# Block-sparse attention and a feed-forward layer on one core: sparse scores with fewer, wider matmuls, and another pace for the feed-forward work

## The chip, the core and the metric

The kernel runs on one core of a Trainium2 chip. A core has TensorE (PE in the profile; its loads of the stationary operand are PEld), VectorE (DVE), ScalarE (ACT), GpSimd (POOL) and SyncE (SP), which run their own instruction streams and wait for each other by semaphores, and 16 DMA engines. The metric is the device time of one execution in microseconds (us), the median over runs.

## The reference

Four batches, eight heads, 768 tokens, head size 64; the tokens form 24 blocks of 32. A query block sees its own block and its two neighbours, the first and the last block, and three sampled blocks; the first and the last query block see everything. A layer norm and a feed-forward layer with residual follow.

```python
scores = scale * np.matmul(q, k.transpose(0, 1, 3, 2))
mask = np.abs(blk_i - blk_j) <= window
mask = mask | (blk_i == 0) | (blk_j == 0) | (blk_i == n_blocks - 1) | (blk_j == n_blocks - 1)
for qb in range(n_blocks):
    for kb in sampled_blocks[qb]:
        mask[qb * block:(qb + 1) * block, kb * block:(kb + 1) * block] = True
attn = softmax(np.where(mask, scores, -1e9))
x = attn @ v                                     # heads joined: 768 x 512 per batch
xn = (x - mu) / np.sqrt(var + 1e-06) * g_ln
out = x + np.maximum(xn @ w_ch1, 0.0) @ w_ch2    # 512 -> 2048 -> 512
```

Inputs are float32. The kernel splits each operand into a high and a low float16 part, so most products are three matmuls: high by high, high by low, low by high.

## The kernel before, in words

**Steps.** Attention works on query tiles t of 128 tokens (four query blocks), 0 to 5 in each of the four batches b, and on half the heads at a time (hg, four heads). One such pair is a sparse step; there are 48. Twice per batch and half two dense steps compute the first and the last query block against all keys. All 64 steps are numbered in program order. A sparse step:

- `gather_k` (L273) copies the keys of the 12 sampled blocks on ACT into a tile `kg`, out of the converted keys `kx`; both come from a pool of three buffers. It is issued two steps ahead.
- `scores` (L317) writes the step's scores, `ps`: 128 partitions, 4 heads, 256 columns each, which are three near blocks (columns 0 to 95), the first and the last block (96 to 159) and three sampled blocks (160 to 255). The four query blocks have different near and sampled keys, so each query block and head has a matmul of its own for each of the three pieces, with 32 queries as the stationary operand: 96 matmuls, 48 with the low query part `ql` (64 contraction rows, two heads side by side) and 48 with the high part `qx` (128 rows, where the other 64 hold the keys' low part).
- `softmax_max`, `softmax_exp`, `split_high` and `split_low` (DVE, ACT) make the probabilities' high and low parts `pw`, and two DMA transposes turn them into `pt`.
- `gather_v` brings the values into `vg`, by DMAs on SP and by indirect DMAs on POOL; `attn_v` (L431) multiplies, two steps later (LAG), into `pa`; `finish` divides.

**Units.** Two query tiles of a batch are a unit, in the order (1, 2), (3, 4), (0, 5); there are 12. When both are finished, `layer_norm` normalises them on DVE and ACT and brings them, turned by DMA, into `xT`. `ffn` (L519) is a generator: 192 matmuls up (`pu`, L532), 96 down (`pd`, L561). Below, U and D are such matmuls, up and down.

**Order.** Nothing is scheduled by a tool: the program order of each engine is that of the main loop (L792). Each turn i issues the scores of step i, the exponentials, the values of step i - 2, and between these, in eight parts (`go`), matmuls of the feed-forward generators. `quota` (L805) says how many: what is still to be done (`need`), divided by the turns until the next unit comes in (`avail`), at most `CAP` = 78. So the feed-forward work of one unit ends as the next unit comes in. Steps 0 to 7 (NPE) have another order and turn the probabilities on PE; then the weights are converted as well.

Of the kernel before, what the change touches and what calls it, by code (L numbers as in the profile page):

```python
# [10 lines left out]
F16 = mybir.dt.float16  # L11
# [15 lines left out]
def sparse_attention_moe(  # L27
# [13 lines left out]
    nc = tc.nc  # L41
    P = 128
    B, NT = qs.shape[0], qs.shape[1]
    H = 8
    D = 64
    HG = 2
    HL = H // HG
    BLK = 32
    NB = NT * 4
    NR = 3  # L50
# [7 lines left out]
    LAG, FFLAG, CAP = 2, 1, 78  # L58
# [1 line left out]
    FFU = 192 + 2 * 16 * 6  # L60

    const = ctx.enter_context(tc.tile_pool(name="const", bufs=1))
    kp = ctx.enter_context(tc.tile_pool(name="kp", bufs=3))
    rawp = ctx.enter_context(tc.tile_pool(name="rawp", bufs=3))
    wfp = ctx.enter_context(tc.tile_pool(name="wfp", bufs=3))
    qp = ctx.enter_context(tc.tile_pool(name="qp", bufs=3))
# [29 lines left out]
            name=nc.get_next_instruction_name(), act_func_set_id=ACT_SET, ins=[], outs=[]  # L96
# [72 lines left out]
    def convert_w(i):  # L169
# [16 lines left out]
        def to_high():  # L186
# [5 lines left out]


    kxs, vgs, qxs, kgs = {}, {}, {}, {}
    vdr = {(b, hg): dr.tile([(NB + 1) * BLK, VW], F16, name=f"vdr{b}_{hg}")
           for b in range(B) for hg in range(HG)}
    vsb = [const.tile([P, H, VR], F16, name="vs")]
# [21 lines left out]

    def convert_k(b, hg, c):  # L220
        if c == 0:
            kxs[b, hg] = kp.tile([P, 2, NB, HL // 2, BLK], F16, tag="kx", name=f"kx{b}_{hg}")
        kx, raw = kxs[b, hg], raws.pop(("k", b, hg, c))
        at = slice(c * NB // 2, (c + 1) * NB // 2)
        for j in range(2):
            rows, other = slice(j * D, (j + 1) * D), slice((1 - j) * D, (2 - j) * D)
            nc.scalar.copy(kx[rows, j, at], raw[rows])
            nc.vector.tensor_sub(kx[other, j, at], raw[rows], kx[rows, j, at])
            yield
# [43 lines left out]
    def gather_k(s):  # L273
        b, t, hg = s.b, s.t, s.hg
        if hg == 0:
            _, got = nc.values_load_multi_w_load_instructions(
                regs[0:1, t * 4 * NR : (t + 1) * 4 * NR], engines=(ET.Activation,), min_val=0,
                max_val=NB - 1,
                skip_runtime_bounds_check_because="every sampled block is a block's number")
            vals[b, t] = got  # L280
        kg = kp.tile([P, 4 * NR, 2, HL // 2, BLK], F16, tag="kg", name=f"kg{b}_{t}_{hg}")
        kgs[b, t, hg] = kg
        for n, val in enumerate(vals[b, t]):
            nc.scalar.copy(kg[:, n], kxs[b, hg][:, :, bass.ds(val, 1)].rearrange("p j o q k -> p j (o q) k"))  # L284
            if n % 4 == 3:
                yield

# [29 lines left out]
    def scores(s):  # L317
        kx, (qx, ql) = kxs[s.b, s.hg], qxs[s.b, s.t]
        kg = kgs[s.b, s.t, s.hg]
        s.ps = ps_s.tile([P, 2, 2, 2 * P], F32, tag="ps", name=f"ps{s.i}")  # L320

        def segments(gr, hl):
            qb = 4 * s.t + gr
            w = min(max(qb - 1, 0), NB - 3)
            j, q = hl % 2, hl // 2
            yield 0, 3, kx[:, j, w : w + 3, q, :]
            yield 3, 2, kx[:, j, 0 : NB : NB - 1, q, :]
            yield 5, 3, kg[:, NR * gr : NR * (gr + 1), j, q, :]

        def put(gr, j, pr, rows, stat, first, last):  # L330
            dst = s.ps[gr * BLK : (gr + 1) * BLK, j, pr, :].rearrange("p (b k) -> p b k", k=BLK)
            for at, n, src in segments(gr, 2 * pr + j):
                nc.tensor.matmul(dst[:, at : at + n], stat, src[rows], start=first, stop=last,  # L333
                                 skip_group_check=True)
                first = False

        for pr in range(2):
            for gr in range(4):
                for j in range(2):
                    rows = slice(j * D, (j + 1) * D)  # L340
                    put(gr, j, pr, rows, ql[rows, 2 * s.hg + pr, gr * BLK : (gr + 1) * BLK],
                        pr == 0, False)
        for pr in range(2):
            for j in range(2):
                for gr in range(4):
                    put(gr, j, pr, slice(0, P), qx[:, j, 2 * s.hg + pr, gr * BLK : (gr + 1) * BLK],
                        False, True)

    def dense_scores(s):
        kx = kxs[s.b, s.hg]  # L350
# [270 lines left out]
    def place(n):  # L621
        return n + (1 if n < NPE else LAG)

    def matmul_scores(s):
        (dense_scores if s.dense else scores)(s)
# [35 lines left out]
    def keys(i):  # L661
        if i < NS and not steps[i].dense and i not in gathered:
            gathered.add(i)
            work(gather_k(steps[i]))
# [48 lines left out]
    first = ORDER[0]  # L713
# [13 lines left out]
    for c in range(2):  # L727
        work(convert_k(0, 0, c))
# [12 lines left out]
    for b in range(1, B):  # L741
        f = next(s.i for s in steps if s.b == b)
        k0, v0 = max(f - 13, NPE + 1), max(f - 11, NPE + 1)
        for hg, i in ((0, k0), (1, f - 4)):
            for c in range(2):
                item(i + c, "b", "raw", lambda b=b, hg=hg, c=c: load_k(b, hg, c),
                     lambda b=b, hg=hg, c=c: convert_k(b, hg, c))
        for kt in range(NT):
            item(v0 + kt, "d", "raw", lambda b=b, kt=kt: load_v(b, kt), lambda b=b, kt=kt: convert_v(b, kt))
# [10 lines left out]
    for n, s in enumerate(order):  # L760
# [4 lines left out]
        else:  # L765
            old = order[n - 3]
            i = place(old.i + 1 if old.dense else old.i)
# [18 lines left out]
    avail = {}  # L786
    for u in units:
        last = max(s.i for s in steps if s.u is u)
        avail[u.i] = last + 2 - 100 * (u.i == 0) if last < NPE else last + LAG + FFLAG
    need = 0  # L790
    i = 0
    while i < NS + LAG + FFLAG + 1 or ffq:  # L792
        s = steps[i] if i < NS else None
# [9 lines left out]
        later = [a for a in avail.values() if a > i]  # L803

        def quota():  # L805
            return min(-(-need // (min(later) - i)), CAP) if later else need

        nff = quota()
        part = [nff * (k + 1) // 8 - nff * k // 8 for k in range(8)]
        wready.update(wdone[: len(wdone) - 1 if i < NPE else None])  # L810
        hook(i, "pre")
        if i < NPE:
# [5 lines left out]
            if i == 0:  # L818
                convert_w(0)
                work(convert_k(0, 1, 0))  # L820
                split_high(s)
                high()
# [53 lines left out]
        else:  # L876
# [3 lines left out]
            def go(k):  # L880
                nonlocal need
                if k == 4:
                    begin(True)
                    if i >= NPE:
                        nff = quota()
                        for m in range(4, 8):
                            part[m] = nff * (m + 1) // 8 - nff * m // 8
                n = part[k]
                for m in range(2):
                    need -= run(n * (m + 1) // 2 - n * m // 2)  # L890
                    low()
                    tick()
                    high()
# [106 lines left out]
```

## Time and profile before

| | |
|---|---|
| time, median of 3 runs | 848.17 us (842.59 to 858.56) |
| the profiled execution | 842.86 us, its span 841.1 us |
| PE matmuls busy | 700.7 us, 13776 matmuls and as many loads |
| DVE, ACT, POOL busy | 496.1, 467.8, 175.6 us |
| mean granted TensorE clock | 0.941 |

Busy time of an engine is the time in which at least one of its instructions ran; small matmuls that run side by side count once. The chain of work is followed back from the last instruction through whatever released each one. "issue" in it is time in which an engine waited for nothing that the profile shows.

### The profile page before, as it was taken

How to read it: one execution, taken by the hardware profiler on the slowest of the kernel's cores; microseconds unless marked ns; L12 is line 12 of the kernel's file. 1: busy time of each engine (PE TensorE's matmuls, PEld its weight loads, DVE VectorE, ACT ScalarE, POOL GpSimd, SP SyncE). 2: the span in 40 equal slices, each digit the busy share in tenths (PEclk: the TensorE clock that was granted, in tenths of full speed). 3: DMA queues.
4: the chain of work that ended last, by engine and by line, in shares of the span. 5: the costliest groups of instructions: out<-in, count | busy, mean ns of one | idle time of the engine just before them, and what ended most of it. 6: DMA issues, size and time to landing. Idle time of an engine off the chain costs nothing.

```text
span 841.1 us, 31767 instructions
## 1 busy us (share of the span) xinstructions
PE 700.7 (83%) x13776; PEld 475.5 (57%) x13776; DVE 496.1 (59%) x900; ACT 467.8 (56%) x1201; POOL 175.6 (21%) x189
## 2 busy tenths in 40 slices
PE   0343397788994798999996999999979999999898
PEld 0242275346652664765854756748637658476483
DVE  4789979847674565656554765646555565443320
ACT  5765654455884565645765774657676565432110
POOL 0145210201151132203131331111333221110000
PEclk9996588988996899999998999999999999999999
DMA  8888555367899669876389789975598796542100
GB/s 292 265 275 238 167 154 163 96 121 218 167 189 242 121 144 220 211 153 187 86 171 225 152 180 236 195 187 110 131 197 161 176 168 146 127 113 40 51 1 26
DMA packets 196043, 136.70 MB, mean 163 GB/s; under 512 B 139584, under 2 KB 174912, under 8 KB 195904
## 3 DMA queue, kind: packets, MB, share of 16 engines
q1 hardware_dynamic: 186496, 110.69, 57.5%
q0 software_dynamic: 8448, 23.44, 11.5%
q8 instruction: 108, 1.77, 0.9%
q10 hardware_dynamic: 960, 0.54, 0.2%
q14 instruction: 31, 0.25, 0.1%
HBM read 89.18 MB, written 12.95 MB: 121 GB/s over the span
## 4 chain that ended last, share of the span: by engine, by line
PE 71%; DVE 14%; ACT 5%; issue 5%; DMA 4%; SPq 0%; ACTq 0%; DVEq 0%
PE pu L532 31%; PE pd L561 25%; PE ps L333 6%; PE pa L440 5%; PE pd L467 2%; DVE wf L175 2%; PE ps L364 2%; DVE st L377 1%; DVE wf L177 1%; DMA xT<-xl 1%; ACT kg L284 1%; DVE w1l L182 1%; DVE wf L173 1%; DVE pw L405 1%; DVE w2l L182 1%
## 5 line engine op out<-in xcount | busy, mean ns | idle before, releaser
L532 PE MATMUL pu<-xT,w1h 128*128 128x256 f16 x1536 | 276.7, 283 | 29.0 <-DMA xT<-xh 16.7
L307 POOL DMA_INDIRECT vg<-vdr,vidx x176 | 174.1, 989 | 551.3 <-PE pa L440 384.4
L532 PE MATMUL pu<-xT,w1l 128*128 128x256 f16 x768 | 217.3, 283 | 0.0
L532 PEld LDWEIGHTS <-w1h 128*128 128x128 f16 x1536 | 153.8, 101 | 51.8 <-DMA xT<-xh 17.0
L386 ACT ACTIVATE ps<-ps,st 128x256 f32<-128x256 f32 (+1 forms) x176 | 85.6, 487 | 123.0 <-DVE st L378 106.3
L561 PE MATMUL pd<-w2h,hh 128*128 128x512 f16 x384 | 147.4, 384 | 0.0
L561 PE MATMUL pd<-w2l,hh 128*128 128x512 f16 x384 | 146.4, 381 | 0.0
L561 PE MATMUL pd<-w2h,hl 128*128 128x512 f16 x384 | 146.3, 381 | 0.0
L284 ACT COPY kg<-kx 128x128 f16 x576 | 123.1, 294 | 9.3 <-issue 7.8
L545 DVE SCALAR_TENSOR_TENSOR hl<-pu,hh 128x512 f16<-128x512 f32 x96 | 65.7, 687 | 91.4 <-ACT hh L544 90.8
L561 PEld LDWEIGHTS <-hh 128*128 128x128 f16 x768 | 71.0, 98 | 81.2 <-issue 4.5
L377 DVE TENSOR_REDUCE st<-ps 128x4 f32<-128x1024 f32 (+1 forms) x64 | 73.8, 1153 | 54.2 <-PE ps L333 27.5
L544 ACT ACTIVATE hh<-pu 128x512 f16<-128x512 f32 x96 | 56.8, 593 | 70.7 <-PE pu L532 70.3
L532 PEld LDWEIGHTS <-w1l 128*128 128x128 f16 x768 | 77.7, 101 | 20.7 <-issue 8.5
L405 DVE TENSOR_TENSOR pw<-ps,pw 128x1024 f16<-128x1024 f32 (+1 forms) x56 | 64.3, 1148 | 35.6 <-ACT pw L398 35.0
L440 PE MATMUL pa<-vg,pt 128*32 128x65 f16 (+1 forms) x4224 | 52.6, 200 | 27.1 <-issue 25.0
L440 PEld LDWEIGHTS <-pt 128*32 128x32 f16 x4224 | 44.4, 99 | 42.8 <-issue 38.7
L561 PEld LDWEIGHTS <-hl 128*128 128x128 f16 x384 | 37.8, 98 | 46.1 <-issue 1.4
L398 ACT CAST pw<-ps 128x1024 f16<-128x1024 f32 (+1 forms) x56 | 52.9, 945 | 0.6
L333 PEld LDWEIGHTS <-ql 64*32 64x32 f16 x2304 | 29.0, 96 | 42.3 <-issue 21.8
L333 PE MATMUL ps<-kx,ql 64*32 64x64 f16 (+1 forms) x1536 | 34.6, 209 | 19.4 <-DVE ql L267 17.0
L267 DVE TENSOR_TENSOR ql<-qr,qx 64x512 f16<-64x512 f32 x44 | 30.1, 685 | 19.0 <-ACT qx L266 18.4
(81 smaller groups left out, 672.2 us busy)
## 6 DMA issues: line engine op xcount, KB each, us to landing
vg<-vdr SPq DMA_DIRECT2D x32, 390.0 KB, 5.0
w2l<-w SPq DMA_DIRECT2D x13, 512.0 KB, 4.5
va<-vdr SPq DMA_DIRECT2D x8, 780.0 KB, 5.3
w2h<-w SPq DMA_DIRECT2D x12, 512.0 KB, 3.5
out<-ot SPq DMA_DIRECT2D x24, 256.0 KB, 4.1
qr<-qs SPq DMA_DIRECT2D x22, 256.0 KB, 4.7
vg<-vdr SPq DMA_DIRECT2D x16, 292.5 KB, 4.4
vdr<-vs SPq DMA_DIRECT2D x36, 130.0 KB, 4.6
```

What stands on the lines that cost most here:

```text
L284: nc.scalar.copy(kg[:, n], kxs[b, hg][:, :, bass.ds(val, 1)].rearrange("p j o q k -> p j (o q) k"))
L307: nc.gpsimd.indirect_dma_start(vg[:, qb - 4 * s.t, 1, :], None, src[:, :], bass.IndirectOffsetOnAxis(ap=vidx[:, qb : qb + 1], axis=0))
L333: nc.tensor.matmul(dst[:, at : at + n], stat, src[rows], start=first, stop=last, skip_group_check=True)
L377: nc.vector.tensor_reduce(out=s.st[:, 0 : s.m], in_=s.parts, axis=AX.X, op=ALU.max)
L386: nc.scalar.activation(to[:, k], s.parts[:, k], AF.Exp, bias=s.st[:, k : k + 1], scale=0.125)
L398: nc.scalar.copy(s.pw[:, 0, 0 : s.n], s.whole)
L405: nc.vector.tensor_sub(s.pw[:, 1, 0 : s.n], s.whole, s.pw[:, 0, 0 : s.n])
L440: nc.tensor.matmul(pa[gr * BLK : (gr + 1) * BLK, hl * 66 : hl * 66 + n], s.pt[:, ch + c, half, gr * BLK : (gr + 1) * BLK], s.vg[:, gr, c, ...
L532: nc.tensor.matmul(ph[:, j * 2 * P : (j + 1) * 2 * P], w[:, c, fs], xT[:, c, k, :], start=n == 0 and j == 0, stop=n == 3 * CT - 1, skip_gr ...
L544: nc.scalar.activation(dh, ph, AF.Relu)
L545: nc.vector.scalar_tensor_tensor(out=dl, in0=ph, scalar=0.0, in1=dh, op0=ALU.max, op1=ALU.subtract)
L561: nc.tensor.matmul(po, x[:, f, cols], w[:, f, :], start=f == 0 and n == 0, stop=f == FT - 1 and n == 2)
```

## The change

**Scores.** The near and the sampled pieces of one query block and head become one matmul of 192 columns: its access pattern has two parts at a fixed distance, one in `kx` and one in `kg`, and its output has two parts in `ps`. For that, keys and gathered keys lie in one tile, `ka`, with three places each, in place of the pool; `kg` has its axes in another order. The first and the last block are the same for all four query blocks, and have one matmul with 128 queries. So there are 16 + 4 matmuls with `ql` and 16 + 4 with `qx`: 40, not 96.

**Pace.** `quota` divides by one turn more, so that about one turn's feed-forward work is left over when the next unit comes in, and is done first. Before turn `avail[1]` = 9 the quota is CAP.

```diff
-    kp = ctx.enter_context(tc.tile_pool(name="kp", bufs=3))
+    KP, KR = HL // 2 * BLK, 3
+    ka = const.tile([P, KR * 2 * (NB + 4 * NR) * KP], F16, name="ka")
+
+    def key_place(n, blocks, lead):
+        at = lead + n % KR * 2 * blocks * KP
+        return ka[:, at : at + 2 * blocks * KP].rearrange("p (j b q k) -> p j b q k", j=2, q=HL // 2, k=BLK)
...
-            kxs[b, hg] = kp.tile([P, 2, NB, HL // 2, BLK], F16, tag="kx", name=f"kx{b}_{hg}")
+            kxs[b, hg] = key_place(len(kxs), NB, 0)
...
-        kg = kp.tile([P, 4 * NR, 2, HL // 2, BLK], F16, tag="kg", name=f"kg{b}_{t}_{hg}")
+        kg = key_place(len(kgs), 4 * NR, KR * 2 * NB * KP)
...
-            nc.scalar.copy(kg[:, n], kxs[b, hg][:, :, bass.ds(val, 1)].rearrange("p j o q k -> p j (o q) k"))
+            nc.scalar.copy(kg[:, :, n], kxs[b, hg][:, :, bass.ds(val, 1)].rearrange("p j o q k -> p j (o q) k"))
...
+        def both(a, b):
+            return bass.AP(tensor=a.tensor, offset=a.offset, ap=[a.ap[0], [b.offset - a.offset, 2], *a.ap[1:]])
+
+        def own(gr, j, pr, rows, stat, last):
             dst = s.ps[gr * BLK : (gr + 1) * BLK, j, pr, :].rearrange("p (b k) -> p b k", k=BLK)
-            for at, n, src in segments(gr, 2 * pr + j):
-                nc.tensor.matmul(dst[:, at : at + n], stat, src[rows], start=first, stop=last,
-                                 skip_group_check=True)
+            w = min(max(4 * s.t + gr - 1, 0), NB - NR)
+            near, got = kx[rows, j, w : w + NR, pr, :], kg[rows, j, NR * gr : NR * (gr + 1), pr, :]
+            nc.tensor.matmul(both(dst[:, 0:NR], dst[:, 8 - NR : 8]), stat[:, gr * BLK : (gr + 1) * BLK],
+                             both(near, got), start=False, stop=last, skip_group_check=True)
+
+        def ends(j, pr, rows, stat, first, last):
+            dst = s.ps[:, j, pr, NR * BLK : (8 - NR) * BLK].rearrange("p (b k) -> p b k", k=BLK)
+            nc.tensor.matmul(dst, stat, kx[rows, j, 0 : NB : NB - 1, pr, :], start=first, stop=last,
+                             skip_group_check=True)
...
-            return min(-(-need // (min(later) - i)), CAP) if later else need
+            if not later:
+                return need
+            return CAP if i < avail[1] else min(-(-need // (min(later) - i + 1)), CAP)
```

The order of the calls in `scores` is now: 4 `ends` with `ql`, 16 `own` with `ql`, 16 `own` with `qx`, 4 `ends` with `qx`.

Here is the start of a score block on PE before (step 36; `ql` is the stationary operand, `kx` or `kg` the moving one, the size is that of the output). One head of one query block takes three pairs:

```order
L333 LDWEIGHTS ql_3_9651
L333 MATMUL ps_10042<-kx_0_5539,ql_3_9651 32x96
L333 LDWEIGHTS ql_3_9651
L333 MATMUL ps_10042<-kx_0_5539,ql_3_9651 32x64
L333 LDWEIGHTS ql_3_9651
L333 MATMUL ps_10042<-kg_3_0_9527,ql_3_9651 32x96
```

And the same step with the change, where the four matmuls for the first and the last block end and those for the near and sampled blocks begin:

```order
L343 LDWEIGHTS ql_3_8072
L343 MATMUL ps_8375<-ka,ql_3_8072 128x64
L343 LDWEIGHTS ql_3_8072
L343 MATMUL ps_8375<-ka,ql_3_8072 128x64
L337 LDWEIGHTS ql_3_8072
L337 MATMUL ps_8375<-ka,ql_3_8072 32x2x96
```

The 192 instructions of a block (a load and a matmul each) have become 80.

The pace is seen best on DVE, which follows PE: an `ot` row (L567) closes a unit's last D, an `hl` row (L545) follows the first U of a unit, and an `rc` row (L424) follows a step's values. Before, around the end of unit 4 and the start of unit 5 (`xl1_5`, L513, is the last piece of unit 5's normalised input on DVE; `st34` and `st35` follow the scores of steps 34 and 35):

```order
L513 TENSOR_TENSOR xl1_5_9383<-xn1_5_9364,xh1_5_9382 128x512
L377 TENSOR_REDUCE st34_9499<-ps34_9402 128x4
L378 TENSOR_SCALAR st34_9499<-st34_9499 128x4
L424 TENSOR_SCALAR rc2_1_0_0_9645<-pa32_9548 128x4
L425 RECIPROCAL rc2_1_0_0_9645<-rc2_1_0_0_9645 128x4
L427 TENSOR_TENSOR x2_1_9646<-pa32_9548,rc2_1_0_0_9645 128x256
L267 TENSOR_TENSOR ql2_3_9651<-qr2_3_9116,qx2_3_9650 64x512 x2
L405 TENSOR_TENSOR pw34_9536<-ps34_9402,pw34_9536 128x1024
L567 SCALAR_TENSOR_TENSOR ot4_1_9682<-pd4_1_9232,x1_4_7021 128x512
L377 TENSOR_REDUCE st35_9801<-ps35_9704 128x4
L378 TENSOR_SCALAR st35_9801<-st35_9801 128x4
L545 SCALAR_TENSOR_TENSOR hl5_9686<-pu5_0_9687,hh5_9685 128x512
```

And with the change, from the scores of step 35 on (line numbers moved: L391 and L392 are the maxima, L438 to L441 `finish`, L581 the `ot` row, L559 the `hl` row):

```order
L391 TENSOR_REDUCE st35_8157<-ps35_8116 128x4
L392 TENSOR_SCALAR st35_8157<-st35_8157 128x4
L438 TENSOR_SCALAR rc2_1_1_0_8286<-pa33_8189 128x4
L439 RECIPROCAL rc2_1_1_0_8286<-rc2_1_1_0_8286 128x4
L441 TENSOR_TENSOR x2_1_8067<-pa33_8189,rc2_1_1_0_8286 128x256
L505 BN_STATS bs2_1_8291<-x2_1_8067 128x6
L506 BN_AGGR mv2_1_8292<-bs2_1_8291 128x2
L235 TENSOR_TENSOR ka_121<-kr3_0_0_7874,ka_121 64x768 x2
L419 TENSOR_TENSOR pw35_8174<-ps35_8116,pw35_8174 128x1024
L581 SCALAR_TENSOR_TENSOR ot4_1_8315<-pd4_1_7876,x1_4_5834 128x512
L511 TENSOR_SCALAR xn2_1_8318<-x2_1_8067,mv2_1_8292 128x512
L559 SCALAR_TENSOR_TENSOR hl5_8321<-pu5_0_8322,hh5_8320 128x512
```

The end of unit 4 and the start of unit 5 have moved from behind the values of step 32 (`pa32`) to behind those of step 33 (`pa33`): one turn later. On PE, between the values of step 31, which complete unit 5's input, and the first U of unit 5, stood 39 D, one score block and one block of values; with the change there stand 69 D, two score blocks and two blocks of values. The counts for the other units of which the prediction speaks, in the same words: unit 2 had 21 D, one score block, one block of values, and has 39 D, two, one; unit 8 had 42 D, one, one, and has 72 D, two, two; unit 11 had 42 D alone, and has 75 D alone.

More of the change, by code (lines that the diff above doesn't have):

```diff
@@ L320, in scores @@
         s.ps = ps_s.tile([P, 2, 2, 2 * P], F32, tag="ps", name=f"ps{s.i}")
[L322 to L330, printed above, removed]
-            dst = s.ps[gr * BLK : (gr + 1) * BLK, j, pr, :].rearrange("p (b k) -> p b k", k=BLK)
-            for at, n, src in segments(gr, 2 * pr + j):
-                nc.tensor.matmul(dst[:, at : at + n], stat, src[rows], start=first, stop=last,
-                                 skip_group_check=True)
-                first = False
+        def both(a, b):
+            return bass.AP(tensor=a.tensor, offset=a.offset, ap=[a.ap[0], [b.offset - a.offset, 2], *a.ap[1:]])
+        def own(gr, j, pr, rows, stat, last):
+            dst = s.ps[gr * BLK : (gr + 1) * BLK, j, pr, :].rearrange("p (b k) -> p b k", k=BLK)
+            w = min(max(4 * s.t + gr - 1, 0), NB - NR)
[6 more added lines that the diff above has]
+                             skip_group_check=True)
+        for pr in range(2):
+            for j in range(2):
+                rows = slice(j * D, (j + 1) * D)
+                ends(j, pr, rows, ql[rows, 2 * s.hg + pr], pr == 0, False)
         for pr in range(2):
@@ L340, in scores @@
                     rows = slice(j * D, (j + 1) * D)
-                    put(gr, j, pr, rows, ql[rows, 2 * s.hg + pr, gr * BLK : (gr + 1) * BLK],
-                        pr == 0, False)
+                    own(gr, j, pr, rows, ql[rows, 2 * s.hg + pr], False)
         for pr in range(2):
@@ L345, in scores @@
                 for gr in range(4):
-                    put(gr, j, pr, slice(0, P), qx[:, j, 2 * s.hg + pr, gr * BLK : (gr + 1) * BLK],
-                        False, True)
+                    own(gr, j, pr, slice(0, P), qx[:, j, 2 * s.hg + pr], True)
+        for pr in range(2):
+            for j in range(2):
+                ends(j, pr, slice(0, P), qx[:, j, 2 * s.hg + pr], False, True)
     def dense_scores(s):
```

## The prediction

> **What bounds the kernel now.** I read the page's first part, then the stages, then what ended the idle time of PE, since PE turned out to be the bound. First the busy times:
>
> ```profile
> PE 700.7 (83%) x13776; PEld 475.5 (57%) x13776; DVE 496.1 (59%) x900; ACT 467.8 (56%) x1201; POOL 175.6 (21%) x189
> ```
>
> PE leads, but 83% hides very different stages. Next the busy times by stretch (PE, loads, DVE, ACT, POOL, then the granted clock, the DMA share and GB/s):
>
> ```profile
> 165.00:267.00 102.00, 80.51 (x1726) 51.24 (x1726) 63.21 (x115) 68.59 (x181) 21.19 (x22) 0.89 0.83 178
> 267.00:340.00 73.00, 62.63 (x1275) 41.70 (x1276) 38.70 (x65) 41.91 (x103) 16.56 (x16) 0.90 0.80 169
> 340.00:440.00 100.00, 99.22 (x1936) 68.38 (x1934) 57.26 (x109) 60.26 (x165) 22.62 (x23) 1.00 0.71 162
> 440.00:520.00 80.00, 70.87 (x1617) 47.38 (x1615) 49.01 (x86) 53.74 (x138) 23.00 (x24) 0.96 0.93 196
> 610.00:665.00 55.00, 46.15 (x1093) 33.33 (x1091) 30.56 (x59) 36.79 (x104) 18.10 (x20) 0.97 0.85 175
> 665.00:790.00 125.00, 124.91 (x2254) 80.75 (x2252) 62.38 (x122) 51.36 (x123) 16.03 (x17) 1.00 0.57 117
> 790.00:841.00 51.00, 44.87 (x294) 29.32 (x292) 7.61 (x11) 4.78 (x8) 0.00 (x0) 0.97 0.07 21
> ```
>
> Before 165 us the weights are converted and PE has only the early steps; I count no gain there. From 340 to 440 and from 665 to 790 PE has no gaps. In the stretches between it idles, and the clock falls below 1.00 in the same stretches. So from 267 us on, whatever PE is spared shortens the kernel, and its gaps are the second thing to look at. The waits view says what ended them:
>
> ```profile
> PE pa L440 <- issue: 25.0, 16, 3.7
> PE pd L467 <- issue: 2.5, 2, 1.7
> PE pu L532 <- DMA xT<-xh: 16.7, 4, 8.5
> PE pu L532 <- issue: 2.4, 2, 1.5
> PE pu L532 <- DMA xT<-xl: 2.3, 3, 0.9
> ```
>
> Two kinds: 19.0 us in which the first U of a unit waits for its normalised input, and 29.9 us of "issue", waits for no semaphore. 6.6 us of the latter lie before 169 us, 23.3 us behind. Where they stand tells what they are. The chain in order of time, around one, and the instruction counts of two stretches that each run from the end of one such gap to the end of the next:
>
> ```profile
> 316.56 1.24 PE ps L333 x76
> 318.55 0.57 PE pa L440 x58
> 319.12 2.25 issue
> 295.50:309.25 13.75, 12.82 (x256) 9.90 (x255) 8.55 (x13) 10.13 (x23) 4.36 (x4) 0.88 0.81 178
> 321.37:332.53 11.16, 9.87 (x255) 5.32 (x255) 7.21 (x12) 8.07 (x14) 4.22 (x4) 1.00 1.05 227
> q8 instruction: 108, 1.77, 0.9%
> ```
>
> The gap opens in the middle of a block of values, and both stretches hold 512 instructions (256 matmuls and 256 loads, to one or two). The queue of instruction packets moved 1.77 MB in 108 packets: 16 KB each, one to 255 of PE's 27552 matmuls and loads. So PE's program arrives in lengths of 256 instructions, and PE stands still where it reaches the end of one before the next has come. Counting 256 back from 321.37, the length before began at 316.66, inside the score block; the next was there 4.7 us later. Over the other gaps the same count gives 3.6 to 7.3 us. A score block followed by a block of values is 384 instructions in little over 2 us: that uses a length up faster than the next one arrives.
>
> **The score block.** Its rows in PE's timeline at step 29, with the U before and behind:
>
> ```profile
> 399.01 0.27 PE L532 MATMUL pu<-xT,w1l 128*128 128x256 f16 x1
> 399.21 0.28 PE L333 MATMUL ps<-kx,ql 64*32 64x96 f16 x11
> 399.67 0.23 PE L333 MATMUL ps<-kg,ql 64*32 64x96 f16 x2
> 399.83 0.27 PE L333 MATMUL ps<-kx,qx 128*32 128x96 f16 x7
> 400.29 0.23 PE L333 MATMUL ps<-kg,qx 128*32 128x96 f16 x2
> 400.45 0.28 PE L532 MATMUL pu<-xT,w1h 128*128 128x256 f16 x1
> 475.41 6.55 PE pu L532 x59
> 782.02 9.19 PE pd L561 x42
> ```
>
> A U of 256 columns takes 6.55 / 59 = 0.11 us, a D 9.19 / 42 = 0.22. The block costs 400.45 - 399.01 - 0.11 = 1.33 us: 0.09 to change from 128*128 to 64*32, 0.46 for the first 48 starts, 0.16 to change to 128*32 (0.04 of it the last matmul's 96 columns, so 0.12 for the change), 0.46, and 0.16 to change back.
>
> After: change 0.09; 4 `ends` of 64 columns at a U's rate, 0.03 each, 0.11; change 0.12; 16 `own` in eight positions of the array, two each of 192 columns (0.083), 0.17; change 0.12; 16 `own` in four positions, four each, 0.33; change 0.12; 4 `ends`, 0.11; no change back, as a U has the same 128*128 shape. Sum 1.17, 0.16 less than 1.33. The unknowns are the loads of the `ends`, which no row shows beside so short a matmul, and the changes:
>
> ```profile
> L532 PEld LDWEIGHTS <-w1h 128*128 128x128 f16 x1536 | 153.8, 101 | 51.8 <-DMA xT<-xh 17.0 <-issue 9.3 <-DMA xT<-xl 1.2
> ```
>
> Such a load, 128 columns in 101 ns, is hidden under every U of 0.11. If all eight were bare, the block would be 8 x 0.10 = 0.81 longer and lose 0.65; if both changes around the `ends` were free, it would save 0.40. Over 40 blocks (8 lie before 165 us): -16 to +26 us; I take the hidden load, the nearer row: **-6**.
>
> **The lengths of 256.** The change takes 56 x 48 x 2 = 5376 instructions out of PE's program, all from its densest places. I laid the two programs out in lengths of 256 and summed each length's work with the durations above (a block of values 0.95). If the next length comes 4.0 us after one is begun, 23 lengths behind 169 us are used up too early, by 23.3 us in all, just the gaps measured. With the change and the same 4.0 us it is 3 lengths, by 1.6 us; with 4.7 us, 7 lengths and 5.1. I leave 4: **-19** (bounds 0 and -23).
>
> The Trainium skill ("Runtime: NRT & Kernel Launch", Instruction fetch mechanics) also has blocks of 256 instructions, but says that the issue rate of the sequencer hides their arrival. Here it doesn't (2.25 us at 319.12); if what I take for arrival were something else, this term would be 0, which is the first rival below.
>
> **The reserve.** Of units 2, 5, 8 and 11, each time the values that complete the unit's input, and its first U with their waits:
>
> ```profile
> 246.24 1.07 PE L440 MATMUL pa<-vg,pt 128*32 128x65 f16 x72
> 267.26 0.39 PE L532 MATMUL pu<-xT,w1h 128*128 128x256 f16 x1 [8.54 <-DMA xT<-xh]
> 436.00 0.91 PE L440 MATMUL pa<-vg,pt 128*32 128x65 f16 x72
> 453.79 0.40 PE L532 MATMUL pu<-xT,w1h 128*128 128x256 f16 x1 [3.97 <-DMA xT<-xh]
> 454.85 0.61 PE L532 MATMUL pu<-xT,w1h 128*128 128x256 f16 x2 [0.46 <-DMA xT<-xl]
> 610.41 0.91 PE L440 MATMUL pa<-vg,pt 128*32 128x65 f16 x72
> 628.28 0.27 PE L532 MATMUL pu<-xT,w1h 128*128 128x256 f16 x1 [2.92 <-DMA xT<-xh]
> 629.57 0.38 PE L532 MATMUL pu<-xT,w1h 128*128 128x256 f16 x2 [0.91 <-DMA xT<-xl]
> 781.11 0.91 PE L440 MATMUL pa<-vg,pt 128*32 128x65 f16 x72
> 792.48 0.28 PE L532 MATMUL pu<-xT,w1h 128*128 128x256 f16 x1 [1.29 <-DMA xT<-xh]
> 793.82 0.38 PE L532 MATMUL pu<-xT,w1h 128*128 128x256 f16 x2 [0.94 <-DMA xT<-xl]
> ```
>
> Unit 5's input is complete 454.85 - 436.91 = 17.9 us after the values of step 31. With the change PE has 69 D (15.1), two score blocks (2.3) and two blocks of values (1.8) there: 19.2 us, just enough, and the 4.43 us go. Unit 8 gets 72 D, two and two, 19.9, for 629.57 - 611.32 = 18.2: 3.83 go. Unit 11 gets 75 D, 16.4, for 793.82 - 782.02 = 11.8: 2.23 go. Together 10.5. Unit 2 gets only 39 D, two score blocks and one of values, 11.7, for 267.26 - 247.31 = 20; its wait shrinks by at most the 18 D and one score block added, 5.1, and only if the attention before it, in a stretch where ACT, DVE and PE are all between 62% and 79% busy, runs earlier by what it is spared. I take 3 of it. **-13.5** (0 to -19). The work itself is only moved: 33 D (7.2 us) more stand behind the last values, which is paid back by as much less before.
>
> **Clock.** From 267 us on the rows above lose (1 - clock) x length: 7.3 + 3.2 + 1.7 + 1.5 = 13.7 us of full speed, all in stretches with gaps. Some of it falls on idle time anyway, some gaps stay: half, **-7** (0 to -14).
>
> At nothing: the ACT copies into `ka`, as many elements as before, on an engine that idles a third of every stretch or more; the one tile, since its program waits on PE for the same copies as before (each block for its own step's gather). If ACT's cover were gone, 576 copies with some 10 ns more each would be 6 us.
>
> Sum: -6 - 19 - 13.5 - 7 = -45.5 against the profiled 842.86: **797 us**. The median of the runs shown is 0.6% above the profiled one; I add nothing for that.
>
> **Rivals.**
> - *The gaps of "issue" stay*, because PE's program is late whatever its density. For it: DMA shares of 0.80 to 0.93 where they occur. Against: they stand in blocks of values close behind score blocks, and with one arrival time for all their sum comes out. Then 797 + 19 + 4 for clock: 820. Chance 0.13.
> - *The next unit's input is late all the same*: the chain behind the values takes longer, since steps become shorter and DVE and SP get to it later. Then 797 + 13 = 810. Chance 0.10, and inside the forecast's range.
> - *The loads of the `ends` lie bare*, and no gain is left: 797 + 6 + 26 = 829, and with half the clock term kept away 833. Against: the U rows. The Trainium skill ("TensorE: Matmul & The Clock Gate", Part 3) lets loads overlap running matmuls only where the row groups differ, which would bare the four `ends` with 128 rows; the U rows, 128 rows each, 0.11 apart with loads of 0.10, disagree. Chance 0.08.
> - *The other side:* attention, not PE, sets the pace up to the last values, by SP's queue and the DMA engines (0.93 from 440 to 520). Then less PE work shortens nothing there, and the 33 D moved behind the last values are added: 842.9 + 7.2 = 850. It decides where a turn gets shorter than its DMA work. Against: 100 and 125 us with PE at 99% while DMA has 0.71 and 0.57. Chance 0.05.
>
> **How the numbers follow.** The forecast of 797, with 782 to 812 for its own bounds, has 0.61, the rivals 0.36, 0.03 is for what I don't see. The range reaches to the first rival and its clock: 782 to 826. A measurement of this kernel tells 2% from no change, that is 826: below it lie the forecast and the first two rivals and some of the rest, 0.87; within 2% the third, the fourth and a remainder, 0.10; above, 0.03.
>
> **What would show it.** The score block on the chain at 1.1 to 1.2 us in place of 1.24 (the chain counts from the U's end). "issue" on PE's values under 10 us in all. No wait for `xT` at units 5, 8 and 11, one of 4 to 8 us at unit 2. From 267 us on PE over 95% busy at a clock of 0.97 or more. The last unit alone about 42 us at the end, as before. I am wrong if the block is above 1.5 us, if gaps of 2 us in blocks of values stay, or if PE waits for `pt` or `vg` between 300 and 700 us.

## The result, and the profile after

The kernel after takes 800.67 us (median of 4 runs, 798.99 to 802.09), the kernel before, on the same chip, 846.29: a ratio of 0.947 (95% interval 0.943 to 0.952). Forecast: 797, in a range of 782 to 826. In the profiled executions 842.86 became 802.09; that of before is over 1.5% above the same kernel's fastest on other chips (829 us) and counts as slow, so that the second pair of traces, further down, is the fairer one. The experiments ran on other chips, where the kernel before took 831 to 834 us; so each is compared by its ratio to before on the same chip, or with a kernel that ran beside it. "On the scale of 846" means that this ratio is applied to the 846 us of the first chip.

The page of after, its busy times and the row of the instruction packets:

```profile
PE 684.5 (86%) x11088; PEld 448.8 (56%) x11088; DVE 493.4 (62%) x900; ACT 465.4 (58%) x1201; POOL 173.8 (22%) x189
q8 instruction: 87, 1.43, 0.8%
```

2688 matmuls and as many loads are gone, and with them 21 packets of 16 KB: 5376 / 21 = 256 instructions each. The stretches (columns as in the prediction's table):

```profile
273.00:340.00 67.00, 66.33 (x1248) 45.47 (x1246) 44.78 (x82) 47.70 (x119) 20.36 (x22) 1.00 1.03 222
...
440.00:520.00 80.00, 77.65 (x1445) 54.95 (x1444) 52.85 (x89) 51.95 (x125) 17.76 (x19) 1.00 1.01 213
...
665.00:758.00 93.00, 93.00 (x1294) 60.85 (x1292) 40.16 (x82) 30.16 (x70) 5.65 (x6) 1.00 0.36 87
```

From unit 2's first U to the last unit PE is 97% busy or more in each stretch, at a clock of 1.00. What PE still waits for behind 273 us (first row: that first U, at 272.8), and that U itself:

```profile
PE pu L546 <- DMA xT<-xh: 3.1, 1, 3.1
PE pu L546 <- DVE hl L559: 1.4, 1, 1.4
PE ps L337 <- issue: 1.3, 3, 0.8
PE pu L546 <- DVE mv L506: 1.2, 1, 1.2
PE pa L454 <- issue: 0.7, 1, 0.7
PE pu L546 <- issue: 0.4, 1, 0.4
272.78 0.28 PE L546 MATMUL pu<-xT,w1h 128*128 128x256 f16 x1 [3.12 <-DMA xT<-xh]
```

Before, the same view had 20.6 us of "issue" there and the prediction's 19.0 of `xT`, 8.5 of them at unit 2. 20.6 us of "issue" have become 2.4, and the `xT` of units 5, 8 and 11 is no longer waited for. The row of `mv` belongs to the "issue" as well: it is one wait, at 341.00, which began at 339.85, and DVE's `mv` had ended at 340.00, 1.0 us before the matmul started; the matmul stands at a boundary of 256 instructions. So 3.6 us is the fuller figure, and `hl`'s 1.4 is the only new wait for DVE. A score block between two U of after:

```profile
381.77 0.38 PE L546 MATMUL pu<-xT,w1h 128*128 128x256 f16 x2
382.09 0.23 PE L343 MATMUL ps<-ka,ql 64*128 64x64 f16 x4
382.25 0.36 PE L337 MATMUL ps<-ka,ql 64*32 64x192 f16 x16
382.54 0.51 PE L337 MATMUL ps<-ka,qx 128*32 128x192 f16 x16
382.99 0.29 PE L343 MATMUL ps<-ka,qx 128*128 128x64 f16 x4
383.11 0.27 PE L546 MATMUL pu<-xT,w1l 128*128 128x256 f16 x1
```

The second of the two U starts at 381.88, so the block costs 383.11 - 381.88 - 0.11 = 1.12 us, 0.21 less than before (1.33).

**The account.** From unit 2's first U to the span's end it was 841.1 - 267.3 = 573.8 us, and is 800.1 - 272.8 = 527.3: 46.5 less. "issue" gives 17.0 (20.6 to 3.6); `xT` at units 5, 8 and 11 gives 10.5, of which DVE's `hl` takes 1.4 back; 33 blocks give 6.9, and one block more lies ahead of unit 2 now, 1.3; the clock gives up to 13.7. Together that is 48.0, a little too much; some of the slow clock probably fell on idle time. Ahead of unit 2 the sign is the other: its first U comes 5.5 us *later*, though its wait is 5.4 shorter (8.54 to 3.12) and the 14 blocks that stood there before are 2.9 shorter. PE's waits from 97 us to that U, after:

```profile
PE px L517 <- DVE xn L511: 22.5, 3, 9.7
PE ps L343 <- DVE pw L419: 3.3, 1, 3.3
```

and before:

```profile
PE px L503 <- DVE xn L497: 17.2, 3, 6.9
```

So, in this pair of executions, the stretch behind unit 2 gained more than the whole forecast, and the one ahead of it gave a part back: 41.0 us between the two spans. The experiments ask three things: are the gaps lengths of 256 instructions, which part of the change brings what, and why is the stretch ahead of unit 2 not shorter.

### The profile page after: what moved, and what is told of

It is laid out like the page before. It is cut to its first block, busy times and chain, and to the rows that moved or that the text cites. A ratio compares the mean times of both kernels' runs of the same rounds, so it can differ in the third digit from the quotient of the medians.

```text
span 800.1 us, 26387 instructions
## 1 busy us (share of the span) xinstructions
PE 684.5 (86%) x11088; PEld 448.8 (56%) x11088; DVE 493.4 (62%) x900; ACT 465.4 (58%) x1201; POOL 173.8 (22%) x189
## 4 chain that ended last, share of the span: by engine, by line
PE 63%; DVE 17%; ACT 7%; DMA 6%; issue 5%; ACTq 1%; SPq 1%; DVEq 0%
PE pd L575 27%; PE pu L546 23%; PE pa L454 4%; PE ps L337 3%; DVE st L391 2%; DMA vdr<-vs 2%; PE pd L481 2%; DVE wf L174 2%; PE ps L343 2%; ACT ka L291 2%; PE ps L378 1%; DVE ka L235 1%; DVE wf L176 1%; DVE pw L419 1%; ACT ps L400 1%
## 5 line engine op out<-in xcount | busy, mean ns | idle before, releaser
L546 PE MATMUL pu<-xT,w1h 128*128 128x256 f16 x1536 | 264.5, 276 | 10.7 <-DMA xT<-xh 3.1
L546 PE MATMUL pu<-xT,w1l 128*128 128x256 f16 x768 | 211.8, 276 | 0.0
L546 PEld LDWEIGHTS <-w1h 128*128 128x128 f16 x1536 | 150.8, 99 | 29.0 <-issue 5.0
L575 PE MATMUL pd<-w2l,hh 128*128 128x512 f16 x384 | 148.1, 386 | 0.0
L291 ACT COPY ka<-ka 128x128 f16 x576 | 123.2, 295 | 8.3 <-issue 6.8
L559 DVE SCALAR_TENSOR_TENSOR hl<-pu,hh 128x512 f16<-128x512 f32 x96 | 65.5, 687 | 71.2 <-ACT hh L558 62.3
L391 DVE TENSOR_REDUCE st<-ps 128x4 f32<-128x1024 f32 (+1 forms) x64 | 73.7, 1152 | 29.8 <-PE ps L378 17.3
L546 PEld LDWEIGHTS <-w1l 128*128 128x128 f16 x768 | 75.9, 99 | 16.6 <-issue 5.8
L454 PE MATMUL pa<-vg,pt 128*32 128x65 f16 (+1 forms) x4224 | 53.1, 200 | 13.8 <-issue 13.8
L405 PE MATMUL ps<-ident,pw 128*128 128x128 f32 x64 | 13.1, 371 | 28.1 <-ACT pw L400 21.6
L581 DVE SCALAR_TENSOR_TENSOR ot<-pd,x 128x512 f32<-128x512 f32 x24 | 16.4, 686 | 32.1 <-PE pd L575 32.0
```

The costliest lines, as they stand in the source:

```text
L291: nc.scalar.copy(kg[:, :, n], kxs[b, hg][:, :, bass.ds(val, 1)].rearrange("p j o q k -> p j (o q) k"))
L391: nc.vector.tensor_reduce(out=s.st[:, 0 : s.m], in_=s.parts, axis=AX.X, op=ALU.max)
L454: nc.tensor.matmul(pa[gr * BLK : (gr + 1) * BLK, hl * 66 : hl * 66 + n], s.pt[:, ch + c, half, gr * BLK : (gr + 1) * BLK], s.vg[:, gr, c, ...
L546: nc.tensor.matmul(ph[:, j * 2 * P : (j + 1) * 2 * P], w[:, c, fs], xT[:, c, k, :], start=n == 0 and j == 0, stop=n == 3 * CT - 1, skip_gr ...
L559: nc.vector.scalar_tensor_tensor(out=dl, in0=ph, scalar=0.0, in1=dh, op0=ALU.max, op1=ALU.subtract)
L575: nc.tensor.matmul(po, x[:, f, cols], w[:, f, :], start=f == 0 and n == 0, stop=f == FT - 1 and n == 2)
```

## Experiments

### Shifting the boundaries

The kernel before, and ahead of everything else:

```diff
+    zw = const.tile([32, 32], F16, name="zw")
+    nc.vector.memset(zw, 0.0)
+    for _ in range(162):
+        nc.tensor.ldweights(zw)
```

> The kernel before with 162 useless weight loads of 32 x 32 at the very start, where PE has nothing to do. They move every boundary of 256 instructions 162 instructions earlier in the program and change nothing else. Theory (PE's program arrives in lengths of 256, one about 4 us after the one before is begun): the gaps behind 169 us stand at other places (none in the middle of the values of step 20 behind 48 matmuls, where the 2.25 us stood; 3 us in the values of step 16, 2.5 us in those of step 52), and their sum falls from 23.3 to about 15 us: 846 - 9 = 837 us (832 to 842). Rival (the gaps belong to blocks of values, or to transfers at those times, not to boundaries): gaps at the same places as before, 23 us of them, 846 us (843 to 849).

825.36 us against 832.09: ratio 0.989 (0.983 to 0.996), 837 on the scale of 846, as forecast. Its chain in order of time (start, duration) where before had gaps in the values of steps 17, 18, 19, 20 and 21:

```profile
280.63 0.65 PE pu L537 x5
281.29 1.33 issue
282.61 6.07 PE pu L537 x54
...
292.90 1.44 issue
...
305.59 3.35 issue
```

The first gap stands among a unit's U, 5 matmuls behind the values of step 17; steps 20 and 21 have none; the third, in step 19, is 3.35 where before had 0.94. The gaps expected in the values of steps 16 and 52 did not come. Counted through the program, each of the three begins at an instruction whose number leaves the same rest on division by 256 as those of before. The same count over all fourteen traces of this case: 50 gaps of more than 0.6 us behind 273 us with no semaphore to wait for, 49 of them at a boundary of 256. The rival is out. Ahead of 273 us it is not so: after's first trace has nine gaps of "issue" between 200 and 261 us, up to 2.9 us long, that stand at no boundary; they are of another kind, and what ended them isn't shown. The size was off: the boundary gaps behind 169 us sum to 7.1, not 15. At the four larger ones the time from the first matmul of one length to that of the next is 3.7, 4.9, 5.3 and 7.1 us, so there is no one arrival time, and a sum worked out with one is an estimate at best. Nor do 16 us of gaps less than in the first trace of before make 16 us of time: behind 169 us the waits for `xT` are 21.5 (19.0 in before), for `pt` 6.2 (1.9), for `hl` 3.0 (none).

### The two halves of the change, one at a time

Scores alone, with the pace of before:

```diff
-            if not later:
-                return need
-            return CAP if i < avail[1] else min(-(-need // (min(later) - i + 1)), CAP)
+            return min(-(-need // (min(later) - i)), CAP) if later else need
```

> The kernel after's scores (40 matmuls, one tile for the keys) with the kernel before's pace of the feed forward. Theory (two causes that add): 40 blocks shorter by 0.21 us each (8.4), the gaps of "issue" behind 169 us fall from 23.3 to some 5.3 (the count of lengths of 256 at 4.0 us, made for this program), the clock gives 4, and the waits for xT at units 5, 8 and 11 stay at some 10 us: 846 - 30 = 816 us (811 to 821). Rival (the reserve is what makes the shorter block pay): what the score block and the gaps spare comes back as longer waits for xT, because PE reaches the unit's end earlier while its input isn't earlier: these waits grow to over 20 us and the time is 828 or more.

816.17 against 832.09: ratio 0.974 (0.964 to 0.985), some 22 us on the scale of 846, not 30. Its waits on PE behind 253 us:

```profile
PE pu L546 <- DMA xT<-xh: 21.8, 4, 9.0
PE pu L546 <- DVE hl L559: 4.5, 7, 1.0
PE pa L454 <- issue: 1.2, 1, 1.2
```

The gaps are all but gone (1.2), more than expected, but the waits for `xT` are 22.8 (1.0 of it for `xl`) where they were 19.0, and 5.7 us of waits for DVE's `hl` (4.5 on U, 1.2 on D) have opened, where before had none. So part of what is spared is waited away, as the rival said, some 9 us of it and not the whole. The mean granted clock, 0.935, is no higher than before's 0.941, but its lowest stretch lies early (0.55 from 60 to 97 us); from 265 us on no stretch is below 0.96, where before had one at 0.89.

Pace alone, with the scores of before (the diff is the change's last hunk, and nothing else):

> The kernel before's scores (96 matmuls) with the kernel after's pace. Theory: no wait for xT at units 5, 8 and 11 and about 3 us at unit 2 (some 14 us of waits less), the gaps of "issue" behind 169 us at 18 us (23.3 before; the same count of lengths for this program), 2 us of clock: 846 - 21 = 825 us (819 to 831). Rival (the pace brings nearly everything, the scores little): 810 or less. Second rival (the gaps swallow the reserve, PE only waits elsewhere): 840 or more.

818.95 against 832.09: ratio 0.980 (0.973 to 0.988), 17 us on the scale of 846. Its waits from unit 2's first U on:

```profile
PE pa L440 <- issue: 7.3, 6, 2.1
PE pu L532 <- issue: 3.9, 3, 2.0
PE pd L561 <- issue: 3.6, 2, 2.4
PE pu L532 <- DMA xT<-xl: 1.5, 1, 1.5
```

No unit waits for its input behind unit 2, and 14.8 us of "issue" stay. The two halves give 22 and 17, together 39, and the whole 45 on its own chip (38 to 39 on the two others, by ratios of 0.954 and 0.955): neither is "nearly everything", and within the intervals they add.

### Two matmuls in place of the access pattern with two parts

```diff
-            nc.tensor.matmul(both(dst[:, 0:NR], dst[:, 8 - NR : 8]), stat[...],
-                             both(near, got), start=False, stop=last, skip_group_check=True)
+            for part, src in ((dst[:, 0:NR], near), (dst[:, 8 - NR : 8], got)):
+                nc.tensor.matmul(part, stat[...], src,
+                                 start=False, stop=last, skip_group_check=True)
```

> The kernel after with near and sampled blocks in two matmuls of 96 columns again, not in one access pattern: 72 matmuls a block instead of 40, the first and last block still with 128 queries. Theory: the block gets 0.15 to 0.25 us longer (32 matmuls more at 10 ns a start, less what their halved columns spare), 6 to 10 us over 40 blocks, and the denser program brings 6 us of gaps of "issue" back (1.6 to 7.5 by the count of lengths at 4.0 us) and 1 of clock: 801 + 15 = 816 us (811 to 821). Rival (the shape changes and the columns set the block's time, not the number of matmuls, and density has nothing to do with the gaps): 801 to 804 us.

805.90 against 832.09: ratio 0.966 (0.959 to 0.973), where after has 0.947 to 0.955. PE's waits from 265 us on:

```profile
PE pa L455 <- issue: 8.1, 5, 2.4
...
PE pu L547 <- issue: 1.0, 2, 0.7
```

9.1 us of gaps stand there, where after's traces have 1.0 to 3.6. But the block itself is only 0.05 us longer than after's (1.28 against 1.23 from U to U, the median of 19), not 0.15 to 0.25: 2 us over 40 blocks. The access pattern with two parts pays by the instructions that it takes out of the program, hardly by the time of the block.

### The first and last block with 32 queries again

```diff
-            nc.tensor.matmul(dst, stat, kx[rows, j, 0 : NB : NB - 1, pr, :], start=first, ...)
+            for gr in range(4):
+                at = slice(gr * BLK, (gr + 1) * BLK)
+                nc.tensor.matmul(dst[at], stat[:, at], kx[rows, j, 0 : NB : NB - 1, pr, :], start=first, ...)
```

> The kernel after with the first and last block in four matmuls of 32 queries each instead of one of 128: 64 matmuls a block instead of 40; near and sampled blocks stay in one access pattern. Theory (a start of 32 columns costs 10 ns, as in the block of before, and the 128-query form saves no time in the block: 32 starts at 10 ns and one more change of shape, against 8 starts of 0.03 and two changes of 0.12): the block stays within 0.08 us of the kernel after's 1.12, and what comes back are gaps of "issue" at boundaries, 4 to 9 us of them behind 169 us in place of 1: 5 to 9 us slower than the kernel after. Rival (the 128-query form carries the saving of the block): block at 1.25 us or more, 10 us or more slower.

799.56 beside the kernel after's 796.35 on the same chip: 3 us slower by the medians, but the intervals overlap (ratios to before 0.958, 0.953 to 0.963, and 0.955, 0.951 to 0.959). A block of it:

```profile
381.93 0.27 PE L548 MATMUL pu<-xT,w1h 128*128 128x256 f16 x1
382.13 0.25 PE L345 MATMUL ps<-ka,ql 64*32 64x64 f16 x16
382.20 0.35 PE L337 MATMUL ps<-ka,ql 64*32 64x192 f16 x16
382.48 0.51 PE L337 MATMUL ps<-ka,qx 128*32 128x192 f16 x16
382.82 0.29 PE L345 MATMUL ps<-ka,qx 128*32 128x64 f16 x16
383.04 0.28 PE L548 MATMUL pu<-xT,w1h 128*128 128x256 f16 x1
```

383.04 - 381.93 = 1.11 from U to U: 0.12 *less* than after, with 24 matmuls more. Its first 16 starts take 0.07 us, 4 ns each, and the next group begins right behind, since the shape stays 64*32; after's four `ends` of 64*128 take 0.16 with the change behind them. So 128 queries in one matmul cost time in the block, 40 x 0.12 = 4.8 us. What they bring is fewer gaps:

```profile
PE pa L456 <- issue: 9.0, 5, 2.7
```

From unit 2 on 9.3 us of "issue" (0.3 on `pd`) stand, where after's trace on the same chip has

```profile
PE pa L454 <- issue: 1.4, 1, 1.4
```

Behind unit 2's first U this execution is 7.4 us longer than after's on that chip (530.0 against 522.6 to the end of the last D): 7.9 of gaps more, 33 x 0.12 = 4.0 less in blocks, and most of the rest more waits for DVE's `hl` (3.8, after 1.1). But its unit 2 began 4.6 us sooner (262.5 against 267.1), for a reason that no run here shows. So the fewer gaps outweigh the longer block behind unit 2, and what the 128 queries are worth in all stays open. That the gaps come back was expected, the shorter block was not: the theory's price of a start (10 ns) was wrong. The rival is out.

### The stretch ahead of unit 2

First both kernels again on one other chip:

> The kernel after once more, unchanged, to have its trace and its time beside the traces of this call, since the times of the kernel before differ by up to 14 us between chips (846 and 832 us medians). Theory: the ratio to before is 0.947 again (0.940 to 0.955), on whatever chip, and gaps of "issue" behind 273 us stand only at boundaries of 256 instructions or are below 0.9 us; the five gaps of 0.5 to 1.2 us in the values of step 14 (3.9 us together), which stood at no boundary, come again if they belong to the program. Rival (they belong to that one execution): they don't come again.

> The kernel before once more, unchanged, for its trace on this chip. Theory (the next length of PE's program arrives some 4 us after one is begun, sooner or later by execution): gaps of "issue" behind 169 us at the same boundaries as in the first trace, with a sum between 10 and 25 us; waits for xT at units 2, 5, 8 and 11 of 16 to 23 us, larger where the gaps are smaller, since PE then comes earlier to an input that is no earlier. Rival: 23 us of gaps and 19 us of waits, in every execution alike.

The kernel after took 794.53 us against 831.26, ratio 0.954 (0.945 to 0.963), before 830.26 in its profiled execution. Before's boundary gaps behind 169 us are 15.8 here, not 23.2, 14 of them where there were 16. Its waits for `xT` sum to 19.0 us once more, not larger with the smaller gaps as expected. Between the two spans lie 36.5 us (828.5 to 792.0), not 41.0, and behind unit 2's first U 33.4, not 46.5: gaps give 11.8 (12.8 to 1.0), `xT` 10.5 less 3.3 of new waits for DVE's `hl` and `ot`, the blocks 8.2, and the clock, 0.99 there before, up to 5.6; 32.8 in all. The first U of unit 2 in after's second trace, in its third (on a third chip), and in before's second:

```profile
265.45 0.39 PE L546 MATMUL pu<-xT,w1h 128*128 128x256 f16 x1 [3.94 <-DMA xT<-xh]
267.13 0.40 PE L546 MATMUL pu<-xT,w1h 128*128 128x256 f16 x1 [3.96 <-DMA xT<-xh]
268.61 0.40 PE L532 MATMUL pu<-xT,w1h 128*128 128x256 f16 x1 [8.50 <-DMA xT<-xh]
```

The two later executions of after have it 5.6 and 7.3 us sooner than the first, so about half of the 13 us lost ahead of it belonged to that execution; the five gaps of 0.5 to 1.2 us in the values of step 14 didn't come again either. But 1.5 to 3.2 us sooner than before, with 4.5 less of wait and 2.9 less in blocks, is still little. From the chain of after's third trace in this stretch:

```profile
214.53 5.19 DMA vdr<-vs
...
252.40 1.00 ACT pw L412
253.43 1.22 DVE pw L419
...
257.08 1.15 DVE st L391
261.29 5.80 DMA xT<-xh
```

No piece of PE of 0.6 us or more stands between 176 and 267 us on this chain. It goes by DVE's maxima (`st`), ACT's and DVE's `pw`, ACT's copies of keys, transfers of values (`vdr`, 9.0 us with its shorter pieces), then the transposes. And the last of these wait their turn on SP's queue, as the queue's timeline shows:

```profile
253.42 4.03 SPq L421 DMA_TRANSPOSE pt<-pw  x2
...
258.70 1.19 SPq L528 DMA_TRANSPOSE xT<-xh  x1
...
261.29 1.22 SPq L528 DMA_TRANSPOSE xT<-xh  x1
```

`xT`'s transposes stand behind `pt` of step 17, which could not start before `pw` of step 17 was there; the first `xh` had been ready since 255.8. Whether they would land sooner ahead of it wasn't tried. Two runs test the reading. The first has 96 matmuls a block up to step 17 (`if s.i < 18:` the three matmuls of before out of the new tile, else the new form):

> The kernel after with the 96 matmuls of before in the steps up to 17, and the 40 matmuls from step 18 on: 14 blocks are 0.21 us longer, all ahead of 260 us. Theory (up to unit 2's first U the attention's chain over DVE, ACT and the transfers sets the pace, not PE, as the chain of waits shows there): the shorter blocks are worth nothing in that part, 0 to 2 us slower than the kernel after. Rival (PE's work counts there as behind it): 14 x 0.21 = 3 us and 3 us of gaps at boundaries, 6 us slower.

798.37 beside 796.35 (ratios to before 0.959, 0.955 to 0.963, and 0.955, 0.951 to 0.959). The medians are at the theory's upper end, but the intervals don't exclude the rival's 6 us. The trace speaks for the theory: with 14 longer blocks ahead of it, unit 2's first U starts at

```profile
267.10 0.39 PE L566 MATMUL pu<-xT,w1h 128*128 128x256 f16 x1 [5.25 <-DMA xT<-xh]
```

as in after's third trace, 267.13; but after's own three traces lie up to 7.3 us apart there, so one trace can't carry much. The second has the old pace ahead of turn 9, and the reserve from there on:

```diff
-            return CAP if i < avail[1] else min(-(-need // (min(later) - i + 1)), CAP)
+            return min(-(-need // (min(later) - i + (i >= avail[1]))), CAP)
```

> The kernel after with the kernel before's pace up to turn 10 (no full turns of the feed forward there), the reserve behind it as it is. In the kernel after the values of step 6 came at 152.4 us, 6.3 later than before, and those of step 16 at 260.5, 8 later. Theory (the full turns ahead of turn 10 push the attention back, and it is the attention that sets the pace up to 265 us): values of step 16 at 250 to 255 us, unit 2's first U 3 to 6 us earlier, 797 us on the scale where the kernel after has 801 (794 to 800). Rival (the early turns only fill time in which PE idles anyway, and the work that is not done there comes back later): 801 to 806 us.

> The kernel after with the kernel before's pace up to turn 10 once more: it took 792.9 us (790.2 to 794.1) where the kernel after took 794.5 (794.0 to 796.8). Theory (the full turns of feed forward ahead of turn 10 hold up step 6's values by some 5 us, and with them the attention that sets the pace there): 1 to 3 us below the kernel after. Rival (the difference was chance): within 0.7 us of it on either side, or above it.

792.92 us beside 794.53 for the kernel after on the second chip, 793.04 beside 796.35 on the third: 1.6 and 3.3 us less, ratios to before 0.951 (0.942 to 0.960) and 0.952 (0.948 to 0.956). Unit 2 begins, in the first and the second of them, and in the run with the new scores and the old pace throughout, at

```profile
262.88 0.28 PE L546 MATMUL pu<-xT,w1h 128*128 128x256 f16 x1 [4.34 <-DMA xT<-xh]
261.19 0.39 PE L546 MATMUL pu<-xT,w1h 128*128 128x256 f16 x1 [5.69 <-DMA xT<-xh]
261.91 0.40 PE L546 MATMUL pu<-xT,w1h 128*128 128x256 f16 x1 [8.95 <-DMA xT<-xh]
```

The first two are 2.6 and 5.9 us sooner than after's trace on the same chip, although unit 2 waits longer there. The direction came as expected both times; the intervals of the ratios overlap those of after, so that the size stays open. It is the fastest version of this study by its medians.

All traces together answer the third question better than that chain does. Where the values of step 7 start, in us:

| | pace of before ahead of turn 9 | pace of after |
|---|---|---|
| 96 matmuls a block | 159.1, 159.5 | 164.3, 163.6 |
| 40 matmuls a block | 155.7, 156.4, 155.3 | 164.7, 160.6, 160.2 |

The program of before with 162 loads ahead has 161.2; the three other variants with the full turns (64 and 72 matmuls, and the larger reserve below) have 159.4 to 159.9. Apart from after's first execution (164.7), the shorter blocks bring these values some 4 us forward, and the full turns of feed forward hold them up by some 5. Unit 2's first U points the same way, with more scatter: with the pace of before it comes at 267.3 and 268.6 with 96 matmuls and at 261.2 to 262.9 with 40; with the pace of after at 267.1 and 268.6 with 96, at 265.5, 267.1 and 272.8 with 40, and at 262.5 to 265.7 in the three variants. So it is the full turns that take back most of what the scores spare ahead of unit 2. That PE's shorter blocks are worth nothing there, the theory of the first of the two runs, holds at most with the full turns.

### A reserve of two turns

`+ 2` in place of `+ 1` in the last line of the pace:

> The kernel after with a reserve of two turns of feed forward instead of one. Theory: of unit 2's wait of 3.1 us nothing is left, the other units had no wait left to lose, and what is put off stands behind the last values, where PE is busy without a gap: 798 us on the scale where the kernel after has 801 (795 to 801). Rival (less feed forward per turn makes the turns too short for DVE, ACT and the transfers, so that attention's own waits open, and the longer tail adds): 802 to 808 us.

799.73 us beside the kernel after's 794.53, ratio to before 0.961 (0.952 to 0.971). Unit 2's wait did not go (3.91 us): its input is set by the chain above, not by how much feed forward is left. The waits for DVE's `hl` behind 169 us are 6.3 us on U and D, where after's trace on that chip has 3.0. The theory was wrong; the rival's direction and price hold, with more waits on `hl` rather than in attention, as far as the traces show it: behind unit 2's first U this one is 2.3 us longer, so half of the 5.2 stays open.

## Why the prediction was right

- **Score block:** 6 us forecast. 0.21 us each, 8.4 over 40 blocks. The groups came as worked out (0.29 and 0.45 for the two groups of `own` with the change behind each, 0.12 for the last `ends`), but for the first `ends`: with their change they take 0.16 where 0.23 was counted. Their loads are not bare, so that the third rival is out. What the working missed is that the `ends` as 32 queries would have been shorter still.
- **Lengths of 256:** 19 forecast, 17.0 behind unit 2 in the first pair of traces, 21.3 behind 169 us if only gaps at boundaries are counted (23.2 to 1.9, the one at 341 us among them). The cause is shown by the shifted program. The one arrival time of 4.0 us behind the term was a fit: at before's gaps the time runs from 3.6 to 7.3 us, as the prediction says itself, and with the measured time of each length in before's trace (its gap taken off) 4.0 us makes, by an estimate, some 15 us of gaps, not 23.3. The term came out because hardly any length of after is used up that fast. The first rival (the gaps stay) is out. The Trainium skill ("Runtime: NRT & Kernel Launch", Instruction fetch mechanics) lets the sequencer's issue rate hide the arrival of the next block of instructions; 49 of 50 gaps at the boundaries, and their moving with 162 loads put ahead, disagree for a program as dense as this. On the second chip only 15.8 us were there to be had behind 169 us, and 1.0 stayed.
- **Reserve:** 13.5 forecast: 10.5 at units 5, 8 and 11 as worked out, less 1.4 of a new wait for DVE (3.3 in the second trace). The wait at unit 2 fell by 5.4, but its first U came no sooner for it, so that the 3 taken there were not gained in that execution. The second rival (input late all the same) is true of unit 2 alone.
- **Clock:** 7 forecast of 13.7, and all of the stretches behind unit 2 are at 1.00. Under-sized: half was kept back for gaps that would stay, and hardly any stayed.
- **The step that failed** is one that the sum didn't contain: the stretch ahead of unit 2 was taken to run on unchanged, or a little earlier by what PE is spared ("runs earlier by what it is spared. I take 3"). Measured by PE's shorter waits and blocks it ran some 13 us longer in the profiled execution (5.5 later, with 5.4 less of wait, 2.9 less in blocks and 1.1 for the one block more), and 3 to 5 in the others (6.3 us sooner by the same sum, 1.5 to 3.2 found). What the prediction put at nothing is the full turns ahead of turn 9, the diff's `CAP`: they hold up the values of step 7 by some 5 us. How much of the 13 us beyond that belongs to the one execution is open. The fourth rival, that attention and not PE sets the pace, was put at 5% for all the time up to the last values; behind unit 2 it doesn't hold. Ahead of it the chain of waits speaks for it, but the shorter blocks with the old pace speak against it as the whole.
- So it is in part luck that the sum of 45.5 stands as close to the 45.6 between the medians (40.8 between the profiled executions, from which it was worked out): two errors of opposite sign. Behind unit 2 it held some 39 (the reserve without unit 2's 3, 33 of the 40 blocks, about 17 of gaps, the clock), and 46.5 came; ahead of it, it held 6, and in the profiled execution 5.5 were lost. And the terms were read off an execution with large gaps and a low clock, on the chip on which the result was then taken: on the second chip 36.5 came. Of what should show, no `xT` wait at units 5, 8 and 11, over 95% busy and the last unit's 41.9 us (754.2 to 796.1) came, and the block is at the lower end; unit 2 waits 3.1, not 4 to 8; and "issue" on PE's values is 13.8 us in all, not under 10, though only 0.7 of it lies behind unit 2, and 2.9 of it, in front of step 10's values at 203 us, is a wait that before did not have.

## What to carry to other kernels

Where a busy engine shows waits for no semaphore, count its instructions from one to the next: a constant number (here 256) points at the arrival of its program, and instructions put ahead of everything, which move the waits, show it. Then an instruction saved in a dense place can be worth more than its own time, even where the larger instruction that replaces it takes longer (here 128 queries for 32: 4.0 us lost in the blocks behind unit 2, 7.9 us of gaps avoided, in one pair of traces). Work held back for the next unit's first wait is worth that wait, once; more of it brings nothing where another engine's chain sets the input's time. And an order that pays in one stretch can cost in another: the full turns that build the reserve took back, ahead of unit 2, most of what the shorter blocks had brought there. Each stretch needs its own answer to what bounds it.

## What the runs showed that was not expected

- The arrival time of the next length differs from length to length and between executions: the same program lost 23.2 us at its boundaries on one chip and 15.8 on another. Behind unit 2 the two traces of before differ by 13.9 us (573.8 and 559.9): 7.8 of it is gaps, and the clock lost, up to 13.7 and 5.6 us, is about the rest. The kernel after, which hardly meets a boundary too early, differed by 4 to 6 us between chips. Whether the chip or the execution decides isn't shown.
- Starts of 64 columns that keep the shape come 4 ns apart in eight positions of the array; 10 ns, the pace of before's block (48 in 0.46 us), was not a price of a start.
